# Half of the reciprocals in the preparation of the S4D modes become an exponential and a Newton step, and three scalings move from VectorE to ScalarE

## The chip, the cores and the metric

One core of one Trainium2 chip runs the whole kernel. Its engines are TensorE (PE, with its weight loads listed as PEld), VectorE (DVE), ScalarE (ACT), GpSimd (POOL) and SyncE (SP, which here only issues DMA transfers); each runs its own instructions in a fixed order and waits for the others through semaphores. The metric is the device time of one execution in microseconds (us), compared by the median of several runs.

## The reference, cut to what matters

The output is the sum of three terms over a layer-normalised input of 2048 tokens by 448 channels: the input itself, a diagonal state-space convolution (S4D), and a gated linear unit (GLU) with 1792 hidden columns.

```python
def _A_ref(u, log_A_real, A_imag, C_real, C_imag, log_dt, D_skip):
    dt = jnp.exp(log_dt)
    A = -jnp.exp(log_A_real) + 1j * A_imag
    C = (C_real + 1j * C_imag) * dt[:, None]
    P = jnp.exp((A * dt[:, None])[:, :, None] * pos[None, None, :])
    K = 2.0 * jnp.einsum("dn,dnl->dl", C, P).real
    ...                                   # y = causal convolution of u with K, by FFT
    return y + u * D_skip[None, None, :]

def _B_ref(x, w_gate, w_up, w_down):
    g = jnp.einsum("bsd,df->bsf", x, w_gate)
    u = jnp.einsum("bsd,df->bsf", x, w_up)
    return jnp.einsum("bsf,fd->bsd", _sigmoid(g) * u, w_down)

x = A_u
xn = _layernorm(x, axis=-1)
return x + _A_ref(xn, ...) + _B_ref(xn, ...)
```

There are 448 channels with 256 complex modes each. Of every mode the kernel needs a decay, exp(-x) with x = dt·exp(log_A_real), a phase per step, A_imag·dt/2π, and the magnitude and angle of C.

## The kernel before

Two streams of work are interleaved on one TensorE. `glu()` runs the GLU in groups of three (last: two) blocks of 128 hidden columns. For each block and each half `t` of the 1024 tokens in work it makes two accumulations of 12 matmuls (`gate`, line 698, tiles `gu`): three products of high and low parts, because 32-bit values are split in two. The tanh of the first (`th`, line 706, ACT), the product with the second (`hf`, line 709, DVE), its high part (`hh`, line 714, ACT) and low part (`hl`, line 716, DVE) follow. After a group come its down projections (`po`, line 811): eight accumulations, each drained by DVE into `acc` (line 816). `gu` and `po` share four PSUM banks, so the first four `gu` accumulations after a group of `po` each wait until DVE has drained one of the last four `po`. The weights of a block are loaded by SP (`wraw`), cast on ACT (`wh`, line 748) and their low part made on DVE (`wl`, line 752); there is one `wraw` buffer.

`conv()` first normalises the input, then prepares the modes (`prep`, two generators, h = 0 and 1, each with 224 channels as 112 partitions by 2·256 values, taken in turns), then generates the kernel K (`kgen`), and last works in the frequency domain (`spectra`). In `prep`, `exp` is an exponential of 514 columns on DVE, written as a polynomial (lines 311 to 318), whose last two columns are `dt`; `pieces` is a reciprocal on DVE in four pieces of 128 columns (line 322). It is called twice per half: on `m3`, for the angle of C, and on `pl` = 1 + tanh(x/2), from which line 373 makes exp(-x) - 1 = -2·tanh/(1 + tanh). `turn` transposes this on PE (line 431) and ACT copies it into `W` (line 433); the magnitudes of C go the same way into `GG`. The phases `U`, `V`, `T` are stored to DRAM as high (ACT, line 393) and low parts (POOL, line 398) by SP, and `phase_load` (line 481) brings them back for the first product of `kgen` (line 531, tile `tr`); `powers` (lines 443 to 448) starts `kgen`'s other input from `W`.

The order of instructions on each engine is not written by hand. A scheduler sets it when the program is built, from the order of emission, priorities (`hp`) and ties (`issue_after`, which puts an instruction behind another one); on the chip each engine then keeps that order, and an instruction that waits holds all behind it on its engine. ACT holds its functions in tables; the program loads one at its start, one for Arctan (line 363) and one at line 365, whose only purpose is to load the table for the rest of the run ahead of the sines.

## Time and profile before

| what | value |
|---|---|
| three timed runs | 732.49, 735.47, 735.87 us (median 735.47) |
| profiled execution, its own time | 737.56 us |
| its span in the trace | 735.7 us |
| mean granted TensorE clock | 0.974 of full speed |
| busy, share of the span | PE 92%, PEld 73%, DVE 76%, ACT 57%, POOL 49% |
| instructions | 19244 |

The span runs from the first to the last instruction; the execution's own time is 1.86 us longer. In a row of the timeline stand the start, the length, engine, line, operation, output<-inputs, the number of instructions merged, and in brackets how long the engine had been idle and what released it. Because consecutive instructions of one engine overlap a little, the time that one costs in a row of them is the distance of starts and not its length. In the table of stages each engine has its busy time and, in brackets, its instructions; behind them stand the granted TensorE clock, the busy share of the DMA engines and their GB/s.

### The profile page before, as it was taken

The page shows a single profiled execution, that of the slowest core. Times are in us where ns is not written, and L with a number is a line of the kernel's source. Part 1 is how long each engine was busy: PE and PEld are TensorE (multiplying, and loading weights), DVE is VectorE, ACT ScalarE, POOL GpSimd, SP SyncE. Part 2 cuts the span into 40 slices and gives each one's busy share as a digit, 9 for nine tenths or more (in the row PEclk, how much of TensorE's full clock was granted, in tenths as well). Part 3 has the DMA queues.
Part 4 walks back from the last instruction along what each step waited for, and adds up shares of the span by engine and source line. Part 5 has one row for each costly group of instructions (what it writes and reads, how often), then busy time and mean ns, then how long its engine had stood idle before and what let it go on. Part 6 is the DMA issues. An engine that isn't in the chain of part 4 may idle for free.

```text
span 735.7 us, 19244 instructions
## 1 busy us (share of the span) xinstructions
PE 680.4 (92%) x7780; PEld 535.5 (73%) x7780; DVE 560.1 (76%) x776; ACT 421.1 (57%) x654; POOL 360.6 (49%) x423
## 2 busy tenths in 40 slices
PE   2898699999999898899999999999999999989995
PEld 2676588878877787556778878877877777767783
DVE  5899995779889899778488988977955555555543
ACT  3656275479777778796686787677553322312320
POOL 2101076846987975776365697575943002530001
PEclk9998899999999999899999999999999999989998
DMA  9957155454334445456942332233259999997745
GB/s 205 230 147 205 29 165 158 162 172 151 84 111 153 144 118 163 133 151 190 261 141 83 103 109 89 82 112 98 63 162 302 252 243 255 249 263 161 194 120 157
DMA packets 102984, 117.24 MB, mean 159 GB/s; under 512 B 13232, under 2 KB 90864, under 8 KB 102896
## 3 DMA queue, kind: packets, MB, share of 16 engines
q1 hardware_dynamic: 78736, 91.87, 45.2%
q10 hardware_dynamic: 21584, 18.24, 9.3%
q0 software_dynamic: 2576, 5.90, 3.1%
q8 instruction: 61, 1.00, 0.6%
q14 instruction: 27, 0.22, 0.1%
HBM read 72.13 MB, written 43.84 MB: 158 GB/s over the span
## 4 chain that ended last, share of the span: by engine, by line
PE 63%; DVE 13%; DMA 7%; ACT 7%; issue 4%; SPq 3%; POOL 1%; ACTq 1%; POOLq 0%; DVEq 0%
PE gu L698 29%; PE po L811 11%; PE sp L893 7%; PE ko L605 5%; PE pv L920 4%; PE tr L531 3%; DVE Et L591 2%; DVE Ft L593 2%; DVE Et L592 2%; SPq L633 1%; ACT S L540 1%; ACT S L538 1%; DVE acc L816 1%; SPq L481 1%; DMA t<-in_c_t_dram 1%
## 5 line engine op out<-in xcount | busy, mean ns | idle before, releaser
L509 POOL TENSOR_TENSOR me<-me,pm 128x32 f32<-128x32 f32 (+1 forms) x168 | 140.3, 835 | 107.4 <-DVE Et L592 96.3
L509 POOL TENSOR_TENSOR mf<-mf,pm 128x64 f32<-128x64 f32 (+1 forms) x112 | 118.2, 1056 | 4.7
L698 PE MATMUL gu<-xh,wh 128*128 128x512 f32 x336 | 102.3, 412 | 7.0 <-DVE acc L816 6.1
L698 PE MATMUL gu<-xh,wl 128*128 128x512 f32 x336 | 98.9, 402 | 0.0
L698 PE MATMUL gu<-xl,wh 128*128 128x512 f32 x336 | 97.5, 396 | 0.0
L591 DVE TENSOR_TENSOR Et<-me,S 128x1024 f32<-128x1024 f32 x56 | 82.8, 1479 | 12.5 <-ACT S L540 10.8
L592 DVE TENSOR_TENSOR Et<-me,S 128x1024 f32<-128x1024 f32 x56 | 79.4, 1417 | 12.3 <-ACT me L522 9.6
L811 PE MATMUL po<-dh,hh 128*128 128x448 f32 x224 | 85.0, 380 | 3.9 <-DVE hf L709 3.1
L698 PEld LDWEIGHTS gu<-xh,wh 128*128 128x128 f32 x336 | 63.2, 195 | 28.9 <-DVE acc L816 6.5
L811 PE MATMUL po<-dl,hh 128*128 128x448 f32 x224 | 83.0, 371 | 0.0
L811 PE MATMUL po<-dh,hl 128*128 128x448 f32 x224 | 82.0, 369 | 0.0
L537 ACT ACTIVATE S<-tr 128x1024 f32<-128x1024 f32 x56 | 57.8, 1032 | 41.8 <-PE tr L531 41.2
L593 DVE TENSOR_TENSOR Ft<-mf,S 128x1024 f32<-128x1024 f32 x56 | 76.8, 1372 | 5.2 <-ACT S L540 2.7
L605 PEld LDWEIGHTS ko<-Et,Ft 128*32 128x32 f32 x3584 | 54.1, 110 | 32.8 <-issue 13.2
L605 PE MATMUL ko<-Et,Ft 128*32 128x64 f32 x3584 | 65.0, 221 | 12.3 <-DVE Ft L593 11.4
L698 PEld LDWEIGHTS gu<-xh,wl 128*128 128x128 f32 x336 | 65.1, 194 | 15.2 <-DVE pl L316 0.7
L698 PEld LDWEIGHTS gu<-xl,wh 128*128 128x128 f32 x336 | 64.5, 192 | 14.0
L714 ACT CAST hh<-hf 128x512 fp32r<-128x512 f32 x56 | 34.9, 623 | 64.5 <-DVE hf L709 58.6
L709 DVE SCALAR_TENSOR_TENSOR hf<-th,gu 128x512 f32<-128x512 f32 x56 | 38.1, 681 | 43.6 <-PE gu L698 39.5
L706 ACT ACTIVATE th<-gu 128x512 f32<-128x512 f32 x56 | 33.7, 602 | 64.4 <-PE gu L698 52.0
L540 ACT ACTIVATE S<-S,hpi 128x1024 f32<-128x1024 f32 x56 | 65.6, 1171 | 0.5 <-issue 0.3
L816 DVE SCALAR_TENSOR_TENSOR acc<-po,acc 128x448 f32<-128x448 f32 x80 | 48.0, 614 | 21.7 <-PE po L811 21.7
(206 smaller groups left out, 1295.6 us busy)
## 6 DMA issues: line engine op xcount, KB each, us to landing
sk_d<-sk ACTq DMA_DIRECT2D x14, 512.0 KB
sx<-x_d SPq DMA_DIRECT2D x32, 224.0 KB
skl<-sk_d SPq DMA_DIRECT2D x16, 448.0 KB
vp<-v_d SPq DMA_DIRECT2D x16, 448.0 KB
v_d<-vt SPq DMA_DIRECT2D x62, 112.0 KB
ph<-ph_d SPq DMA_DIRECT2D x224, 24.0 KB
wt_d<-wh SPq DMA_DIRECT2D x9, 512.0 KB
wt_d<-wl SPq DMA_DIRECT2D x9, 512.0 KB
```

Source lines behind the costliest of these rows:

```text
L509: ins = nc.gpsimd.tensor_tensor(m[:, :, w + a : 2 * w : n], m[:, :, a:w:n], par(base + i).unsqueeze(2).to_broadcast([128, 4 * DC, w // n]) ...
L537: nc.scalar.activation(rows(cs), pv, AF.Abs)
L540: sins[:] = [nc.scalar.activation(cs, cs, AF.Sin, scale=-TWO_PI, bias=hpi)]
L591: v.tensor_tensor(Et[:, :, :, 32:64], two(me[:, :, 32:64]), S[:, 1::-1], ALU.mult)
L592: v.tensor_tensor(Et[:, :, :, 0:32], two(me[:, :, 0:32]), S[:, 1:3, :, ::-1], ALU.mult)
L593: fts[:] = [v.tensor_tensor(Ft, two(mf), S[:, 3:5], ALU.mult)]
L605: mm = nc.tensor.matmul(ko[32 * j : 32 * j + 32, sl], Ft[:, cc, DC * h + 4 * q + j], Et[:, cc, DC * h + 4 * q + j], start=(k == 0), stop=( ...
L698: glu_mm[:] = [nc.tensor.matmul(ps, a_, b_, start=(n == 0), stop=(n == len(mm) - 1))]
L709: marks[1] = v.scalar_tensor_tensor(hf, th, 1.0, pgu[1], ALU.add, ALU.mult)
L811: glu_mm[:] = [nc.tensor.matmul(po, a_[:, bs], w_, start=(n == 0), stop=(n == 3 * fc - 1))]
L816: v.scalar_tensor_tensor(acc[:, b], po, 0.5, acc[:, b], ALU.mult, ALU.add)
L893: mm = nc.tensor.matmul(to, tb[:kk, t, 64 * c : 64 * c + 64], rhs, start=True, stop=True, skip_group_check=True,)
```

## The change

In both halves of `prep`:

- The reciprocal of 1 + tanh(x/2) goes. With t = tanh(x/2), 2/(1 + t) equals 1 + exp(-x), so ACT computes exp(-x) with `AF.Exp` and adds 1 (`rc`, in the buffer of `ki`), and DVE improves it by one Newton step (two instructions) before the last product.
- `dt` is scaled on ACT by four constants (`hdt`, now four pairs of columns), and ACT uses these as scales: for the tanh, the exponential, the phases (`aim`, was line 386) and the magnitudes (`a3`, was line 419).
- The first product of the polynomial (line 314) becomes an ACT instruction.
- Tanh and Exp are emitted earlier, in the section of `exp`, and Arctan is tied behind the last of them.

```diff
@@ exp
-        v.tensor_scalar(pl, fr, cs[7], None, ALU.mult)
+        nc.scalar.activation(pl, fr, AF.Identity, scale=cs[7])
@@ prep
-        hdt = pool.tile([CP, 2], F32, name="hdt", bufs=2)
+        hdt = pool.tile([CP, 4, 2], F32, name="hdt", bufs=2)
         part = lambda t, i: t[:, N * i : N * i + N]
-        dt = lambda i: ex[:, 2 * N + i : 2 * N + i + 1]
...
         yield from exp(ex, ki, fr, pl)
-        v.tensor_scalar(hdt, ex[:, 2 * N :], 0.5, None, ALU.mult)
+        for i, c in enumerate((0.5, -1.0, 1.0 / TWO_PI, 2.0)):
+            nc.scalar.activation(hdt[:, i], ex[:, 2 * N :], AF.Identity, scale=c)
+        fr, pl, ki = fr[:, : 2 * N], pl[:, : 2 * N], ki[:, : 2 * N]
+        rc = ki.bitcast(F32)
+
+        def scaled(to, src, c, func=AF.Identity):
+            for i in range(2):
+                nc.scalar.activation(part(to, i), part(src, i), func, scale=hdt[:, c, i : i + 1])
+
+        scaled(fr, ex, 0, AF.Tanh)
+        scaled(rc, ex, 1, AF.Exp)
+        nc.scalar.activation(pl, fr, AF.Identity, bias=one[:CP])
+        exps[:] = [nc.scalar.activation(rc, rc, AF.Identity, bias=one[:CP])]
         yield
...
-        nc.scalar.activation(w3, w3, AF.Arctan)
+        with tc.issue_after(exps[0].ins):
+            nc.scalar.activation(w3, w3, AF.Arctan)
...
-        fr, pl, ki = fr[:, : 2 * N], pl[:, : 2 * N], ki[:, : 2 * N]
-        for i in range(2):
-            nc.scalar.activation(part(fr, i), part(ex, i), AF.Tanh, scale=hdt[:, i : i + 1])
-        nc.scalar.activation(pl, fr, AF.Identity, bias=one[:CP])
-        pieces(pl)
-        v.scalar_tensor_tensor(pl, fr, -2.0, pl, ALU.mult, ALU.mult)
+        v.scalar_tensor_tensor(pl, pl, -0.5, rc, ALU.mult, ALU.mult)
+        v.scalar_tensor_tensor(rc, pl, 2.0, rc, ALU.add, ALU.mult)
+        v.scalar_tensor_tensor(pl, fr, -1.0, rc, ALU.mult, ALU.mult)
         yield
         turn(pl, W1s[0], h)
...
-        for i in range(2):
-            v.tensor_scalar(part(fr, i), part(aim, i), 1.0 / TWO_PI, dt(i), ALU.mult, ALU.mult)
+        scaled(fr, aim, 2)
         nc.scalar.copy(ki, fr)
...
-        for i in range(2):
-            v.tensor_scalar(part(a3, i), part(a3, i), 2.0, dt(i), ALU.mult, ALU.mult)
+        scaled(a3, a3, 3)
```

The scheduler's order moves with it. Line numbers of the changed kernel are 7 higher from `kgen` on, and differ in `prep`.

On DVE, around the last four drains of the first group of `po`, before (tiles ending in 377 and 389 are `a3` of h = 0 and 1):

```order
L417 TENSOR_TENSOR a_377<-a_377,b_378 112x512
L322 RECIPROCAL pl<-pl 112x128 x8
L816 SCALAR_TENSOR_TENSOR acc<-po,acc 128x448 x2
L417 TENSOR_TENSOR a_389<-a_389,b_390 112x512
L260 SCALAR_TENSOR_TENSOR z<-z,ve 128x8
L816 SCALAR_TENSOR_TENSOR acc<-po,acc 128x448 x2
```

and in the changed kernel, from the Newton step of h = 0 on (tiles ending in 380 and 392 are the angles `w3` of h = 0 and 1):

```order
L380 SCALAR_TENSOR_TENSOR pl<-pl,ki 112x512
L261 SCALAR_TENSOR_TENSOR ys<-z,ys 128x8
L381 SCALAR_TENSOR_TENSOR ki<-pl,ki 112x512
L263 SCALAR_TENSOR_TENSOR zs<-mv,ys 128x8
L382 SCALAR_TENSOR_TENSOR pl<-fr,ki 112x512
L380 SCALAR_TENSOR_TENSOR pl<-pl,ki 112x512
L385 SCALAR_TENSOR_TENSOR w_380<-w_380,s_381 112x512
L381 SCALAR_TENSOR_TENSOR ki<-pl,ki 112x512
L823 SCALAR_TENSOR_TENSOR acc<-po,acc 128x448 x3
L385 SCALAR_TENSOR_TENSOR w_392<-w_392,s_393 112x512
L382 SCALAR_TENSOR_TENSOR pl<-fr,ki 112x512
```

Before, the fifth to eighth drains stand behind eight reciprocals; now the fifth to seventh stand behind both halves' Newton steps and behind line 385, which needs the Arctan of h = 0 from ACT.

On ACT, the stretch with the two later table loads, before:

```order
L363 ACT_TABLE_LOAD
L363 ACTIVATE w_380<-w_380 112x512
L363 ACTIVATE w_392<-w_392 112x512
L296 COPY x1ab<-ko 128x448
L300 DMA x_d<-x1ab 64x2x448
L748 CAST wh<-wraw 128x1024
L296 COPY x1ab<-kp 128x448
L300 DMA x_d<-x1ab 64x2x448
L365 ACT_TABLE_LOAD
```

and now, from the scalings of `dt` of h = 1 on:

```order
L354 ACTIVATE hdt<-ex 112x2 x4
L300 DMA x_d<-x1ab 64x2x448
L364 ACTIVATE pl<-fr,one 112x512
L365 ACTIVATE ki<-ki,one 112x512
L360 ACTIVATE fr<-ex,hdt 112x256 x2
L360 ACTIVATE ki<-ex,hdt 112x256 x2
L364 ACTIVATE pl<-fr,one 112x512
L365 ACTIVATE ki<-ki,one 112x512
L375 ACT_TABLE_LOAD
L375 ACTIVATE w_380<-w_380 112x512
L375 ACTIVATE w_392<-w_392 112x512
L360 ACTIVATE fr<-aim,hdt 112x256 x2
```

The Arctans, ahead of the cast of a weight block before, now stand behind it and behind all scalings, tanhs and exponentials of both halves. There are three table loads in each program.

On SP, the end of the stores of phases (`w_380` and `w_392` are the low parts of the last phase of h = 0 and 1, which POOL makes one after the other) and the first loads of them, before:

```order
L399 DMA ph_d<-w_380 112x2x256
L394 DMA ph_d<-P_115 112x2x256
L633 DMA wraw<-in_B_w_gate_dram 64x128
L631 DMA wraw<-in_B_w_up_dram 128x3x128
L399 DMA ph_d<-w_392 112x2x256
L633 DMA wraw<-in_B_w_up_dram 64x128 x2
L639 DMA rd<-in_B_w_down_dram 128x448
L755 DMA wt_d<-wh 128x1024
L755 DMA wt_d<-wl 128x1024
L481 DMA ph_1103<-ph_d 12x2x256 x8
L481 DMA ph_1104<-ph_d 12x2x256 x8
```

and now:

```order
L407 DMA ph_d<-w_380 112x2x256
L640 DMA wraw<-in_B_w_up_dram 64x128 x2
L407 DMA ph_d<-w_392 112x2x256
L646 DMA rd<-in_B_w_down_dram 128x448
L762 DMA wt_d<-wh 128x1024
L488 DMA ph_1111<-ph_d 12x2x256 x8
L488 DMA ph_1112<-ph_d 12x2x256 x8
L762 DMA wt_d<-wl 128x1024
```

The last loads of the weight block `wraw` now stand ahead of the store of `w_392`, and the loads of phases ahead of the store of `wl`; both programs have the phase loads behind the store of `wh`.

More of the change, by code (lines that the diff above doesn't have):

```diff
@@ L1103, in s4d_glu_kernel @@
     xq, psc, raws, acl, marks, slots, pqs = list(x_first), [], [], [], [None, None], {}, []
-    W1s, GGs, act = [], [], []
+    W1s, GGs, act, exps = [], [], [], []
     gens = [conv(), glu()]
```

## The prediction

> **What bounds the kernel now.** I read the table of waits for TensorE first (the releaser, total us, times, longest), up to 120 us, because `prep` runs there.
>
> ```profile
> PE gu L698 <- DVE acc L816: 6.1, 1, 6.1
> PE po L811 <- DVE acc L816: 0.8, 1, 0.8
> ```
>
> TensorE waits twice for VectorE's drains of `po`, together 6.9 us. The table of stages tells whose fault that is:
>
> ```profile
> core 0: us, PE busy (x) PEld busy (x) DVE busy (x) ACT busy (x) POOL busy (x), PEclk, DMA share, GB/s
> 60.00:80.00 20.00, 16.11 (x78) 13.60 (x62) 19.73 (x39) 14.77 (x24) 0.20 (x1) 0.83 0.59 161
> 80.00:100.00 20.00, 13.92 (x52) 11.05 (x51) 19.57 (x37) 6.66 (x14) 2.62 (x2) 0.83 0.18 58
> 100.00:120.00 20.00, 20.00 (x97) 16.56 (x96) 14.31 (x15) 10.48 (x22) 15.44 (x14) 1.00 0.67 205
> 120.00:140.00 20.00, 20.00 (x112) 17.73 (x111) 15.98 (x25) 12.25 (x16) 17.26 (x21) 1.00 0.37 119
> ```
>
> From 60 to 100 us VectorE is full (39.3 of 40 us) and TensorE is not; ScalarE has 13 us free between 80 and 100. Behind 100 us TensorE is full. So 60 to 100 us is bound by VectorE, and what follows by TensorE. The timeline of VectorE, then of TensorE, shows the place:
>
> ```profile
> 73.14 0.61 DVE L816 SCALAR_TENSOR_TENSOR acc<-po,acc 128x448 f32<-128x448 f32 x1
> 76.69 0.61 DVE L816 SCALAR_TENSOR_TENSOR acc<-po,acc 128x448 f32<-128x448 f32 x1
> 80.30 6.62 DVE L322 RECIPROCAL pl<-pl 112x128 f32<-112x128 f32 x8
> 86.85 1.09 DVE L816 SCALAR_TENSOR_TENSOR acc<-po,acc 128x448 f32<-128x448 f32 x2
> ```
>
> ```profile
> 81.01 0.37 PE L811 MATMUL po<-dh,hl 128*128 128x448 f32 x1
> 87.46 1.65 PE L698 MATMUL gu<-xh,wh 128*128 128x512 f32 x3 [6.08 <-DVE acc L816]
> 93.51 0.39 PE L698 MATMUL gu<-xr,wh 128*128 128x512 f32 x1
> 95.36 0.84 PE L698 MATMUL gu<-xh,wh 128*128 128x512 f32 x3
> 96.03 0.39 PE L698 MATMUL gu<-xr,wh 128*128 128x512 f32 x1
> ```
>
> The fifth drain stands behind all eight reciprocals; the first `gu` needs its bank and starts 0.61 us after the drain begins. The wait costs more than 6.08 us: the 14 matmuls from 87.46 to 93.51 (rows between left out) take 6.05 us, while 3 take 0.67 us from 95.36 to 96.03, so 14 would take 3.1. Restarting slowly costs 2.9 us. (The waits of 0.8 us leave no such mark.)
>
> The Trainium skill, "TensorE: Matmul & The Clock Gate", Part 1, has the array at half clock until about 3.4 us of sustained work have passed; by it the slow start would cost 1.7 us and not 2.9. The stretch here is longer, and I keep the trace's 2.9.
>
> **VectorE, removed and added.** The costs of one in a run are distances of starts.
>
> ```profile
> L314 DVE TENSOR_SCALAR pl<-fr 112x514 f32<-112x514 f32 x2 | 0.8, 418 | 0.0
> L419 DVE TENSOR_SCALAR a<-a,ex 112x256 f32<-112x256 f32 x4 | 1.2, 341 | 0.0
> 90.72 1.28 DVE L373 SCALAR_TENSOR_TENSOR pl<-fr,pl 112x512 f32<-112x512 f32 x2
> 92.53 1.13 DVE L386 TENSOR_SCALAR fr<-aim,ex 112x256 f32<-112x256 f32 x4
> ```
>
> Gone: eight reciprocals 6.55 (80.30 to 86.85), two of line 314 0.7 (0.8 less overlap), four of line 386 1.05, four of line 419 1.15, together 9.45 us. New: four Newton instructions of the form of line 373, 1.21 a pair (90.72 to 91.93): 2.4 us. Net 7.0 us less on the engine that is full. Line 373 itself stays.
>
> **ScalarE, added, and now waited for.** What moves is long on ScalarE, and the new order puts the fifth to seventh drains behind line 385, which needs the first Arctan.
>
> ```profile
> 66.06 1.28 ACT L363 ACT_TABLE_LOAD   x1
> 67.36 0.63 ACT L363 ACTIVATE w<-w 112x512 f32<-112x512 f32 x1
> 71.62 0.20 ACT L365 ACTIVATE junk<-w 112x1 f32<-112x1 f32 x1
> 71.73 0.71 ACT L377 ACTIVATE m<-w,qpi 112x512 f32<-112x512 f32 x1
> 74.70 0.89 ACT L370 ACTIVATE fr<-ex,hdt 112x256 f32<-112x256 f32 x2
> 75.50 0.71 ACT L380 ACTIVATE w<-w,hpi 112x512 f32<-112x512 f32 x1
> 72.96 0.60 ACT L714 CAST hh<-hf 128x512 fp32r<-128x512 f32 x1
> 76.91 1.33 ACT L371 ACTIVATE pl<-fr,one 112x512 f32<-112x512 f32 x2
> ```
>
> ```profile
> 66.51 0.68 DVE L716 TENSOR_TENSOR hl<-hf,hh 128x512 fp32r<-128x512 f32 x1
> 68.63 0.69 DVE L318 SCALAR_TENSOR_TENSOR ex<-pl,ki 112x514 f32<-112x514 f32 x1
> ```
>
> The end of `exp` (line 318, twice 0.6 us) now follows directly on the `hl` of 66.51, so it ends at about 68.3; one polynomial instruction more ahead of that place pays for the two of line 314 gone. From there ScalarE has, until the first Arctan is done: eight scalings of `dt` at 0.11 (71.62 to 71.73; at most its length, 0.20): 0.9. Two pairs of Tanh at 0.80 (74.70 to 75.50), 1.6. Two pairs of Exp: no row shows an Exp; bounds are a pair of Tanh of the same shape, 0.80, and two 512-column instructions, 1.33; the first is the nearer, 1.6. Four additions of 1 at 0.62: 2.5. One `hh` cast: 0.6. Table load: 1.3 (66.06 to 67.36). Arctan: 0.6. Sum 9.1, so 77.4 us; eight of these read what ScalarE has just written, which I bound by 0 and 0.3 each and take at 0.1: 78.2 (77.4 to 80). Then VectorE does line 385 and one Newton instruction, 1.2, and the fifth drain begins at 79.4. TensorE may start `gu` 0.6 later, at 80.0 (to 82).
>
> TensorE itself comes there at 81.2 (81.01 plus one 0.2 step) less the 0.8 wait, since the first drains no longer stand behind lines 376, 416 and 379: 80.4. Four small transposes now come first, about 0.4, which it did later before. So the wait of 6.08 and that of 0.8 vanish, or leave up to 1.2 us, too short to be slow after. Gain on TensorE: 6.08 + 0.8 + 2.9 = 9.8, with an allowance of 0.5 for a rest: 9.3 us.
>
> On the other side, the Trainium skill, "ScalarE: Activation LUTs", What ACT_TABLE_LOAD costs, has 1.28 us for a load and 1.38 of draining besides. The rows show 1.30 from the start of the load to the next instruction. By the page the first Arctan would come 1.4 us later, the fifth drain at 80.8, and TensorE would wait some 0.5 us: the gain would be 8.8 for 9.3.
>
> The hidden parts: the four scalings of phases and magnitudes, 0.8 a pair on ScalarE, 3.2 in all, fall into the 13 us that it has free between 80 and 100; without that cover they would delay the phases by as much. The cast of the next block's weights needs the buffer of the block that starts here, four accumulations of 12 steps of 0.227 us or 11 us after the start, and is no earlier wanted.
>
> **What is late next.** `kgen`'s start must come forward as well, or TensorE meets its first product (`tr`) too early.
>
> ```profile
> 94.16 1.83 DVE L401 TENSOR_TENSOR aim<-fr,ki 112x512 f32<-112x512 f32 x2 [0.43 <-ACT ki L387]
> 98.54 3.92 POOL L398 TENSOR_TENSOR aim<-aim,p 112x512 fp32r<-112x512 f32 x2 [3.70 <-DVE fr L405]
> 109.26 1.15 POOL L775 TENSOR_TENSOR dl<-rd,dh 128x448 fp32r<-128x448 f32 x1
> 110.37 1.74 POOL L398 TENSOR_TENSOR w<-w,P 112x512 fp32r<-112x512 f32 x1
> 112.49 1.11 SPq L633 DMA_DIRECT2D wraw<-in_B_w_up_dram  x2
> 115.37 1.05 ACT L748 CAST wh<-wraw 128x1024 fp32r<-128x1024 f32 x1 [4.75 <-DMA wraw<-in_B_w_up_dram]
> 118.12 7.82 SPq L481 DMA_DIRECT2D ph<-ph_d  x16
> ```
>
> POOL makes the low phases without a break from 98.54 to 112.1. On SP the last weights wait for its last but one and last result, the cast at 115.37 for them, the store of `wh` for the cast, and the phase loads for that store. VectorE is 7.0 us less busy but now waits about 2 us for ScalarE around the Arctan, and each later hand-over costs up to 0.43 (94.16); I take 5.5 us earlier for POOL (0 to 7). In the new order the weights stand ahead of the last store, so they wait for one POOL instruction less and for the `dl` ahead of it (109.26 to 112.1): 2.9 us more. So phases come 8.4 us earlier (3 to 10), about what TensorE gains. If the change stopped there, the lesser, 8.4, is what reaches 140 us.
>
> **What reaches the end.** The rest of every engine's order stays almost the same, so later stages shift as a whole, where nothing else bounds them.
>
> ```profile
> PE ko L605 <- DVE Ft L593: 11.1, 10, 2.2
> ```
>
> ```profile
> 220.00:260.00 40.00, 35.98 (x507) 29.14 (x506) 37.59 (x40) 31.12 (x47) 33.49 (x33) 0.96 0.49 155
> ```
>
> From 100 to 520 us TensorE waits 11.1 us for VectorE's `Ft`; these waits depend on how the streams meet and may take some of the gain. I leave 0.9 us for that: 7.5 us. In the profiled execution's terms 735.7 goes to 728.2 (its own time 737.56 to 730.1). The profiled run lies 2.1 us above the median of the timed ones, so I subtract from the median: 735.47 - 7.5 = 728.0.
>
> **Rivals.**
> - ScalarE takes VectorE's place. If the self-waits cost 0.3 and more and the scalings of `dt` 0.2, the Arctan ends near 82, `gu` starts near 84, TensorE waits over 3 us and starts slowly again (2.9). Left: 87.5 - 84 + 0.8 = 4.3, or 731.2. For it: the chain is serial and one instruction late holds three drains. Against: every duration in it stands in a row.
> - The gain is real but taken back by `kgen`, whose VectorE is near full at 220 to 260 us (37.6 of 40), POOL at 33.5: if the 11.1 us of `Ft` waits grow by half, 5.5, then 2 us remain: 733.5. Against: those streams start earlier too.
> - Slower: the hand-overs between ScalarE and VectorE in the phases' chain. VectorE's order from line 385 to line 416 and ScalarE's from the second table load on wait for each other some 25 times where both were loosely coupled. At 0.43 apiece that is 10.8 us against the 7.0 saved; TensorE then stands at `tr` until the phases come, some 4 us later than before, slow start (2.9) included 6: 741.5. It decides from 0.3 us each, if nothing overlaps. Against: most of them have other work in between.
> - That the change does not do what it says: an Exp outside Tanh's table would add loads. Both programs have three. No chance of its own.
>
> **Chances and range.** Forecast 0.65, with its own range 725.5 to 731; ScalarE's chain 0.16; taken back 0.12; slower 0.07. A measurement of this kernel tells 0.5%, or 3.7 us, from no change, so 731.8 and 739.1 are the bounds. Faster: nearly all of the forecast and about two thirds of the next, 0.75. Slower: 0.06. The same: 0.19. The range goes from 725.0, where TensorE's 9.8 us arrive whole, to 733.5 and leaves out about 0.15.
>
> **What would show it.** Right: no wait of `gu` for `acc` over 1 us near 81 us; first `gu` at 80.4 to 82; TensorE at full clock from 80 to 100; the first Arctan done near 78; `ph` loads near 110; three table loads; every later stage some 8 us earlier. Wrong: VectorE idle before line 385 until 81 or later with TensorE waiting on `acc`; `tr` waiting for `ph`; or a stage behind 140 us that takes longer than before.

## The result, and the profile after

| what | before | after |
|---|---|---|
| timed runs, median (range) | 733.98 us (731.60 to 737.25, 6 runs) | 723.93 us (722.09 to 728.76, 6 runs) |
| ratio, with its 95% interval | | 0.9857 (0.9824 to 0.9889) |
| profiled execution, its own time (span) | 737.56 us (735.7) | 724.73 us (722.9) |
| busy DVE, ACT, PE | 560.1, 421.1, 680.4 us | 553.6, 428.6, 676.9 us |
| mean granted TensorE clock | 0.974 | 0.980 |

The change makes the kernel 10 us faster. Medians here and below leave out three executions that took 950 us and more (two of e13, one of the kernel before). The forecast was 728.0 us, 7.5 us less, in a range that began at 725.0: the direction was right and the gain too small.

The table of TensorE's waits up to 120 us, after (releaser, total us, times, longest), no longer has `acc` in it:

```profile
PE po L818 <- DVE hf L716: 2.9, 1, 2.9
PE po L818 <- ACT hh L721: 1.4, 1, 1.4
```

The table of stages, after:

```profile
60.00:80.00 20.00, 17.09 (x77) 15.23 (x72) 17.45 (x36) 14.79 (x33) 0.20 (x1) 0.83 0.57 153
80.00:100.00 20.00, 20.00 (x96) 16.57 (x96) 20.00 (x28) 17.93 (x38) 10.11 (x5) 1.00 0.38 115
100.00:120.00 20.00, 18.28 (x81) 14.56 (x80) 14.38 (x24) 11.40 (x21) 13.62 (x19) 1.00 0.54 162
```

Between 80 and 100 us TensorE was busy for 13.92 us at a clock of 0.83; now it is busy for all 20.00 at full clock. VectorE stays full there, but with other work. The timelines of ScalarE, VectorE and TensorE, after, at the place of the old wait:

```profile
73.91 0.90 ACT L360 ACTIVATE ki<-ex,hdt 112x256 f32<-112x256 f32 x2
...
76.06 1.28 ACT L375 ACT_TABLE_LOAD   x1
77.35 1.15 ACT L375 ACTIVATE w<-w 112x512 f32<-112x512 f32 x2
```

```profile
78.01 0.69 DVE L385 SCALAR_TENSOR_TENSOR w<-w,s 112x512 f32<-112x512 f32 x1 [1.25 <-ACT w L375]
78.62 0.69 DVE L381 SCALAR_TENSOR_TENSOR ki<-pl,ki 112x512 f32<-112x512 f32 x1
79.22 1.68 DVE L823 SCALAR_TENSOR_TENSOR acc<-po,acc 128x448 f32<-128x448 f32 x3
```

```profile
79.90 0.96 PE L705 MATMUL gu<-xh,wh 128*128 128x512 f32 x3
...
83.20 0.39 PE L705 MATMUL gu<-xr,wh 128*128 128x512 f32 x1
```

The first Arctan is done at 78.0, line 385 and one Newton instruction follow, the fifth drain starts at 79.22, and TensorE starts `gu` 0.68 us after it without a gap, 7.56 us earlier than before (87.46) and at full pace. On SP's queue the loads of the phases, after, start 7.8 us earlier than before (118.12):

```profile
110.30 7.77 SPq L488 DMA_DIRECT2D ph<-ph_d  x16
```

So the two times that the forecast is added up from came out nearly to the microsecond. What it missed lies elsewhere. This table follows three landmarks (starts of instructions of VectorE, from the traces; `Ft` is line 593 before, `yy` line 904) through two profiles of each kernel, the second ones from the runs e8 and e7:

| us | first `Ft` | 21st `yy` | last `yy` | from 21st to last `yy` | span |
|---|---|---|---|---|---|
| before, first | 132.8 | 640.1 | 706.4 | 66.4 | 735.7 |
| before, second | 134.0 | 640.6 | 706.8 | 66.2 | 735.9 |
| after, first | 124.5 | 632.6 | 694.0 | 61.4 | 722.9 |
| after, second | 124.3 | 631.0 | 693.8 | 62.7 | 722.6 |

Up to 640 us the change gains 8.5 us (means of the two); from there to the last `yy` another 4.2, in a stage of `spectra` that the diff does not touch: from the 21st `yy` on every engine has the same instructions in the same order in both traces. The first profile of before shows what happens in it, on VectorE, on GpSimd, and on TensorE:

```profile
641.54 0.39 DVE L907 TENSOR_TENSOR yy<-pd 128x224 f32<-128x224 f32 x1
...
648.73 0.98 DVE L906 TENSOR_TENSOR yy<-yy 128x224 f32<-128x224 f32 x1
649.74 2.43 DVE L907 TENSOR_TENSOR yy<-pd 128x224 f32<-128x224 f32 x1
...
652.63 0.61 DVE L905 TENSOR_TENSOR pd<-kc,sp 128x448 f32<-128x448 f32 x1
```

```profile
648.43 1.04 POOL L758 CAST wh<-wraw 128x1024 fp32r<-128x1024 f32 x1 [6.20 <-PE sp L893]
649.55 2.37 POOL L759 TENSOR_TENSOR wl<-wraw,wh 128x1024 fp32r<-128x1024 f32 x1
```

```profile
653.38 1.72 PE L955 MATMUL pv<-vp,wf 64*32 64x224 f32 x16 [2.67 <-DVE pd L905]
655.03 1.65 PE L698 MATMUL gu<-xh,wh 128*128 128x512 f32 x3
...
659.89 0.92 PE L698 MATMUL gu<-xh,wh 128*128 128x512 f32 x3
```

Line 907 takes 0.39 us by itself. Where POOL subtracts at the same time it takes 2.43 and ends 0.25 us after POOL does (652.17 and 651.92). `pd` stands behind it, TensorE waits 2.67 us for `pd` and then works slowly until about 660. In the first profile after, POOL meets the same products:

```profile
642.57 0.61 DVE L912 TENSOR_TENSOR pd<-kc,sp 128x448 f32<-128x448 f32 x1
643.11 1.21 DVE L913 TENSOR_TENSOR yy<-yy 128x224 f32<-128x224 f32 x1
...
644.77 2.05 DVE L914 TENSOR_TENSOR yy<-pd 128x224 f32<-128x224 f32 x1
```

```profile
643.03 1.04 POOL L765 CAST wh<-wraw 128x1024 fp32r<-128x1024 f32 x1 [7.03 <-DMA wraw<-in_B_w_up_dram]
644.16 2.42 POOL L766 TENSOR_TENSOR wl<-wraw,wh 128x1024 fp32r<-128x1024 f32 x1
```

But here the last `pd` has started before POOL does, and TensorE does not wait. In this profile GpSimd's cast waits for its weights to land (the releaser in brackets; in the first profile of before its wait ended with TensorE's `sp`), while TensorE comes when its own stream gets there; the two meet or miss each other.

### The profile page after: what moved, and what is told of

Read it like the earlier page. It is cut to its first block, busy times and chain, and to the rows that moved or that the text cites. A ratio compares the mean times of both kernels' runs of the same rounds, so it can differ in the third digit from the quotient of the medians.

```text
span 722.9 us, 19254 instructions
## 1 busy us (share of the span) xinstructions
PE 676.9 (94%) x7780; PEld 532.5 (74%) x7780; DVE 553.6 (77%) x760; ACT 428.6 (59%) x678; POOL 361.9 (50%) x423
## 4 chain that ended last, share of the span: by engine, by line
PE 63%; DVE 11%; ACT 9%; DMA 6%; issue 4%; SPq 2%; POOL 2%; ACTq 1%; POOLq 0%; DVEq 0%
PE gu L705 27%; PE po L818 14%; PE sp L900 7%; PE ko L612 5%; PE pv L927 4%; PE tr L538 3%; DVE Ft L600 2%; DVE Et L599 2%; DVE Et L598 2%; ACT S L547 1%; ACT S L545 1%; ACT S L544 1%; SPq L640 1%; DVE pm L452 1%; DMA ph<-ph_d 1%
## 5 line engine op out<-in xcount | busy, mean ns | idle before, releaser
L516 POOL TENSOR_TENSOR me<-me,pm 128x32 f32<-128x32 f32 (+1 forms) x168 | 138.2, 823 | 104.4 <-DVE Et L599 87.9
L516 POOL TENSOR_TENSOR mf<-mf,pm 128x64 f32<-128x64 f32 (+1 forms) x112 | 121.1, 1081 | 4.7
L705 PE MATMUL gu<-xh,wh 128*128 128x512 f32 x336 | 100.8, 407 | 0.9 <-ACT xh L221 0.7
L705 PE MATMUL gu<-xh,wl 128*128 128x512 f32 x336 | 97.3, 397 | 0.0
L600 DVE TENSOR_TENSOR Ft<-mf,S 128x1024 f32<-128x1024 f32 x56 | 78.7, 1405 | 5.6 <-ACT S L547 2.7
L723 DVE TENSOR_TENSOR hl<-hf,hh 128x512 fp32r<-128x512 f32 x56 | 47.7, 851 | 18.2 <-ACT hh L721 18.2
```

Source lines behind the costliest of these rows:

```text
L516: ins = nc.gpsimd.tensor_tensor(m[:, :, w + a : 2 * w : n], m[:, :, a:w:n], par(base + i).unsqueeze(2).to_broadcast([128, 4 * DC, w // n]) ...
L600: fts[:] = [v.tensor_tensor(Ft, two(mf), S[:, 3:5], ALU.mult)]
L705: glu_mm[:] = [nc.tensor.matmul(ps, a_, b_, start=(n == 0), stop=(n == len(mm) - 1))]
L723: v.tensor_tensor(hl, hf, hh, ALU.subtract)
```

## The experiments

All times are medians of the timed runs; each batch had its own runs of the kernel before on the same chip.

| run | what | us | before | ratio (95%) |
|---|---|---|---|---|
| e1 | Newton alone | 732.16 | 733.41 | 0.9973 (0.9947 to 0.9999) |
| e2 | eight reciprocals left out | 727.79 | 733.41 | 0.9912 (0.9883 to 0.9941) |
| e3 | before, late `wl` on VectorE | 737.68 | 733.41 | 1.005 (1.0027 to 1.0074) |
| e4 | after, the same | 729.17 | 733.41 | 0.9937 (0.9905 to 0.997) |
| e5 | scalings alone | 733.29 | 734.89 | 0.9975 (0.9951 to 1.0) |
| e6 | after, reciprocals tied | 723.89 | 734.89 | 0.9857 (0.9826 to 0.9888) |
| e7 | after, again | 724.11 | 734.89 | 0.9864 (0.9824 to 0.9903) |
| e8 | before, again | 733.45 | 734.89 | 0.9996 (0.9972 to 1.0019) |
| e9 | before, late `wl` in four | 735.11 | 734.53 | 0.9993 (0.9963 to 1.0023) |
| e10 | after, the same | 726.26 | 734.53 | 0.9874 (0.9836 to 0.9911) |
| e11 | after, Arctan later | 725.22 | 734.53 | 0.9873 (0.9833 to 0.9913) |
| e12 | e6 and e10 together | 725.19 | 734.53 | 0.986 (0.9815 to 0.9904) |
| e13 | e9, stores off ScalarE | 732.53 | 734.75 | 0.9987 (0.9955 to 1.0019) |
| e14 | e10, stores off ScalarE | 723.45 | 734.75 | 0.9846 (0.9805 to 0.9887) |
| e15 | e12, stores off ScalarE | 724.32 | 734.75 | 0.9844 (0.9801 to 0.9887) |

### e1, e2, e5: the parts of the change, one at a time

e1 has the exponential and the Newton step, and with them the earlier Tanh and Exp and the tie of the Arctan; line 314 and the scalings stay on VectorE. The core of it:

```diff
...
-        pieces(pl)
-        v.scalar_tensor_tensor(pl, fr, -2.0, pl, ALU.mult, ALU.mult)
+        v.scalar_tensor_tensor(pl, pl, -0.5, rc, ALU.mult, ALU.mult)
+        v.scalar_tensor_tensor(rc, pl, 2.0, rc, ALU.add, ALU.mult)
+        v.scalar_tensor_tensor(pl, fr, -1.0, rc, ALU.mult, ALU.mult)
```

> Only the reciprocal is replaced (Exp on ScalarE, one Newton step); line 314 and all scalings stay on VectorE. VectorE loses 6.55 - 2.4 = 4.2 us of work instead of 7.0. Theory A (the place: what is gained is TensorE's wait for the drains behind the reciprocals, 6.9 us, and its slow restart, 2.9): the wait of gu for acc near 81 us is gone and the gain is that of the whole change, 8 to 11 us against before. Theory B (the amount of work on the full engine): 4.2/7.0 of the gain, about 6 us.

e2 is the kernel before without the reciprocals of `pl` (the decay is then not divided by 1 + t).

```diff
-        pieces(pl)
```

> The kernel before with the eight reciprocals of 1 + tanh left out (the modes' decay is then wrong), everything else left; ScalarE gets no new work and no drain stands behind the Arctan. Theory A: no wait of gu for acc near 81 us, a gain of 8 to 11 us as in the change, so the longer chain on ScalarE costs nothing. Theory B: 6.6 us. If ScalarE's chain cost the change something, this kernel would be faster than the change by 1 us or more.

e5 moves only line 314 and the scalings to ScalarE; the reciprocals stay.

```diff
-        v.tensor_scalar(pl, fr, cs[7], None, ALU.mult)
+        nc.scalar.activation(pl, fr, AF.Identity, scale=cs[7])
...
-            v.tensor_scalar(part(fr, i), part(aim, i), 1.0 / TWO_PI, dt(i), ALU.mult, ALU.mult)
+        scaled(fr, aim, 2)
...
-            v.tensor_scalar(part(a3, i), part(a3, i), 2.0, dt(i), ALU.mult, ALU.mult)
+        scaled(a3, a3, 3)
...
```

> Only the scalings by dt (and line 314) go to ScalarE; all sixteen reciprocals stay on VectorE. Theory A (what reaches the later stages is the lesser of two advances, that of the first gate products after the drains and that of the phases' last stores; both follow VectorE's work ahead of them): VectorE has 0.7 + 1.05 + 1.15 = 2.9 us less, of which the 0.7 and the first scaling stand ahead of the fifth drain, so TensorE still waits at least 4.5 us for it near 81 us, starts slowly again, and the time falls by 1 to 3 us, ratio 0.996 to 0.999. Theory B (the 4 us that the whole change gains beyond leaving the eight reciprocals out come from the scalings alone): the time falls by 4 us or more, ratio 0.9945 or less. Theory C (ScalarE's longer chain costs what VectorE saves): ratio 1.000 or above.

Measured: 1.3, 5.6 and 1.6 us off the medians, where the whole change takes off 10. e1 gains far less than either sum for it; e2's 5.6 is nearer to its second sum, 6.6. The timelines of e1 on TensorE, on SP, on VectorE and on ScalarE, and its stage from 140 us on (compare the row of before behind it), tell why:

```profile
78.74 0.86 PE L708 MATMUL gu<-xh,wh 128*128 128x512 f32 x3
```

```profile
115.05 6.50 SPq L491 DMA_DIRECT2D ph<-ph_d  x16
```

```profile
118.46 1.23 DVE L762 TENSOR_TENSOR wl<-wraw,wh 128x1024 fp32r<-128x1024 f32 x1 [2.39 <-ACT wh L758]
```

```profile
123.19 0.83 ACT L458 ACTIVATE pm<-pm,one 128x640 f32<-128x640 f32 x1 [1.84 <-DVE pm L455]
...
125.01 0.99 ACT L547 ACTIVATE S<-tr 128x1024 f32<-128x1024 f32 x1
```

```profile
140.00:180.00 40.00, 36.83 (x498) 29.37 (x500) 38.53 (x42) 30.21 (x45) 29.49 (x30) 0.96 0.53 173
```

```profile
140.00:180.00 40.00, 39.85 (x454) 32.26 (x453) 32.68 (x37) 28.73 (x43) 20.25 (x25) 1.00 0.49 156
```

TensorE starts `gu` at 78.74, even earlier than in the whole change, but the phases come only 3.1 us earlier (115.05 for 118.12), and a third input of `kgen`, the powers (tile `pm`), not at all. On VectorE half of them stand behind `wl`, which waits 2.39 us for its cast; the first ten are done at 123.15, for 122.99 before. ScalarE waits for them and takes up what `tr` brings (`tr` starts at 121.72) only at 125.01. From 140 to 180 us TensorE then loses 3 us of work in waits, and the 21st `yy` is 1.3 us earlier than in the first profile of before (638.7 for 640.1). e2 leaves another one behind, on SP and on TensorE:

```profile
107.91 6.43 SPq L480 DMA_DIRECT2D ph<-ph_d  x16
```

```profile
74.06 0.47 PE L810 MATMUL po<-dh,hh 128*128 128x448 f32 x1 [1.75 <-DVE acc L815]
...
82.69 0.94 PE L697 MATMUL gu<-xh,wh 128*128 128x512 f32 x3
```

The phases come 10.2 us earlier, but `gu` only 4.8, since without the new order of VectorE the drains still stand behind other work of the preparation (1.75 us wait, `gu` at 82.69); the 21st `yy` is 5.4 us earlier than there (634.6). In e5 the drains stand behind both sets of reciprocals, `gu` starts later than before, at 88.39, and the 21st `yy` is 0.5 us earlier; the median lies within what the first theory expected. Side by side, with e11 from below (us earlier than in the first profile of before; the powers by the end of their first ten instructions on VectorE):

| run | first `gu` | phase loads | powers | 21st `yy` |
|---|---|---|---|---|
| e1 | 8.7 | 3.1 | -0.2 | 1.3 |
| e2 | 4.8 | 10.2 | 8.2 | 5.4 |
| e5 | -0.9 | 2.7 | 1.8 | 0.5 |
| e11 | 8.9 | 3.7 | 5.8 | 5.6 |
| the change | 7.6 | 7.8 | 7.2 | 7.4 |

What arrives is close to the least of the three advances; in e11 it is 1.9 us more. The prediction had counted the first two alone, and these do not tell e1 from e11: `gu` and phases agree within 0.6 us, the powers are 6.0 apart and the 21st `yy` 4.3. The parts together are worth more (10) than one by one (1.3 and 1.6), because each alone leaves at least one of the three behind.

### e3, e4: the late subtraction moved to VectorE

```diff
-                            nc.gpsimd.tensor_tensor(wl, raw, wh, ALU.subtract)
+                            v.tensor_tensor(wl, raw, wh, ALU.subtract)
```

> The kernel before, with the low parts of the reloaded weights of the second half (line 759, five instructions) made on VectorE instead of POOL, so that no POOL instruction of 2.4 us can slow VectorE's products at 650 us. Theory A says that 5.0 of the 12.8 us between the two profiled executions come from there and not from the preparation: no wait of pv there over 1 us, 731 to 733 us, that is 0 to 4 us below the runs of before of the same chip, and less spread. Rival: the 5 us are not a matter of chance but come with the earlier preparation; then this kernel stays at before's time.

> The changed kernel with the same edit of line 759. Theory A: 721 to 724 us, 8 to 10 us below the kernel before with this edit (e3_late_before), which is what the preparation alone is worth: 9.8 us on TensorE less what later waits take. Rival (the late 5 us belong to the change): 12 us or more below it.

Measured: 4.3 us more than before, and 5.2 more than the change; both times are above what was expected, and the two kernels are 8.5 us apart, as the first theory had it. The edit does not take the collision away but puts a wait in its place; VectorE and TensorE of e3:

```profile
653.67 1.23 DVE L759 TENSOR_TENSOR wl<-wraw,wh 128x1024 fp32r<-128x1024 f32 x1 [7.55 <-POOL wh L758]
```

```profile
656.11 3.51 PE L955 MATMUL pv<-vp,wf 64*32 64x224 f32 x48 [5.87 <-DVE pd L905]
```

VectorE now stands 7.55 us for POOL's cast, which waits for the weights, and TensorE 5.87 us for what is queued behind. The trial says nothing about the collision itself, only that this stage charges what VectorE loses there.

### e7, e8: both kernels once more

No edit; a second profile and more times of each.

> The changed kernel unaltered, once more, for a second profile and more times. Theory A (the stage near 650 us loses about 4.5 us in those executions in which POOL's subtraction for the low weights of the second half falls on VectorE's products for pv, by chance of the transfers): times in two groups some 4 us apart as the kernel before has them; the landmarks of this profile agree with those of the first within 1 us up to 640 us, whichever group it is in; a TensorE wait over 1.5 us near 645 to 650 us stands in the profile only if it is in the upper group. Mean ratio 0.986 to 0.990. Theory B (the change moves the two apart for good): one group of times, ratio 0.984 to 0.986.

> The kernel before unaltered, for a second profile. Ratio 1.000 within 0.003. Theory A (the stage near 650 us differs by execution): if this profile's time lies near 732, TensorE has no wait over 1 us for pv near 653 us and the last 80 us are some 4 us shorter than in the first profile; if it lies near 737 the wait of 2.67 us is there again. Theory B (the wait is a fixed part of the kernel before, and the two groups of times come from elsewhere): the wait is there at either time.

The landmarks stand in the table above: up to 640 us the two profiles of a kernel agree within 1.2 us (before) and 1.6 us (after). e8's profile, at 737.82, has the wait again, TensorE:

```profile
654.24 1.72 PE L955 MATMUL pv<-vp,wf 64*32 64x224 f32 x16 [2.94 <-DVE pd L905]
```

Over all batches there are 109 runs of the kernel before, 729.8 to 740.1 us, with a median of 734.28, and 12 of the changed kernel, 721.47 to 730.65, with a median of 724.11. Their spreads are alike, the difference of medians is 10.2 us. The rival's one narrow group of times for the changed kernel is not there. Both profiles of before (737.56, 737.82) lie in the slower quarter of its runs, both of the change (724.73, 724.40) near its median; so some 3 of the 13 us between the spans are how the executions fell.

### e9, e10: the late subtraction in four pieces

```diff
-                            nc.gpsimd.tensor_tensor(wl, raw, wh, ALU.subtract)
+                            for i in range(4):
+                                nc.gpsimd.tensor_tensor(wl[:, :, i], raw[:, :, i], wh[:, :, i], ALU.subtract)
```

> The kernel before, with POOL's subtraction for the low weights of the second half (one instruction of 2.37 us) in four of a quarter of the size; TensorE's, VectorE's and ScalarE's order stays the same. Theory A (in the slower executions near 650 us VectorE's products for pv stand still for as long as one instruction of POOL on the same memory lasts): line 907 takes at most 0.39 + 0.7 us there for 2.43, TensorE's wait for pv falls under 1.5 us, the upper group of times (736 and more) thins out or goes, median 731.5 to 732.5, ratio 0.995 to 0.998. Theory B (VectorE stands still until POOL is done with all four): nothing changes, ratio 0.999 to 1.002. Theory C (it was the transfers, not POOL): as B, but line 907 keeps its 2.4 us even where no POOL instruction runs.

> The changed kernel with the same split. If theory A of the split holds: one group of times near 723 (the three in twelve of 726 and more go), ratio to the kernel before 0.984 to 0.986, and against the split kernel before 9 us less, which is then what the change is worth where neither collides (7.5 was forecast). If the change owes over 3 us of its gain to rarer collisions: only 6 to 7 us less than the split kernel before. If the split does nothing: 724 with the two groups as before.

Measured: no gain in either kernel. In neither profile do the pieces meet the products, so what they cost there isn't shown; but e9 is slow in its profile all the same (738.27 us, 66.5 us from the 21st to the last `yy`), from another wait. ScalarE and TensorE of e9:

```profile
658.46 4.26 ACTq L240 DMA_DIRECT2D out_dram<-ac  x3
662.76 0.60 ACT L706 ACTIVATE th<-gu 128x512 f32<-128x512 f32 x1 [12.93 <-DMA out_dram<-ac]
...
664.64 0.96 ACT L927 COPY vt<-pv 128x448 f32<-128x448 f32 x2
```

```profile
665.22 1.76 PE L894 MATMUL sp<-skl,tb 128*64 128x224 f32 x8 [3.75 <-ACT vt L927]
```

Three output stores are issued on ScalarE's queue and take 4.26 us; `th` and the copy `vt` stand behind them, and TensorE waits 3.75 us for the bank that `vt` frees. The same wait stands in e12 (3.29 us), in e2 (2.98), and in the second profile after (1.68). A theory of one collision near 650 us falls: there are at least two waits, and an execution meets the one, the other or (e10, with 1.5 and 1.4 us) both.

### e13, e14, e15: both late waits taken away

To the four pieces comes that SyncE and GpSimd alone issue the first output stores (`out` takes the engines as its last argument):

```diff
...
-                    out(ac[:, 4 * q : 4 * q + 4], 4 * q, h)
+                    out(ac[:, 4 * q : 4 * q + 4], 4 * q, h, (nc.sync, nc.gpsimd))
```

> The kernel before with both late waits taken away that the profiles show between 640 and 665 us: POOL's subtraction in four pieces, and the first output stores issued by SyncE and GpSimd alone, so that ScalarE's th and vt no longer stand behind three of them (1.7 to 4.3 us of issue). Theory A (the last stage is the same work in both kernels and differs only by these two waits): from the 21st yy to the last one 60.5 to 62 us for 66.4, and one narrower group of times, median 729.5 to 731.5, ratio 0.993 to 0.997. Theory B (the stores or the pieces only move the wait to SP or POOL): 63 us and more in that stage, ratio 0.998 to 1.003.

> The changed kernel with the same two edits. Theory A (the change is worth what is gained before 640 us, 8.4 us in the mean of the profiles, and what the timed runs show beyond that is how the last stage falls): the last stage as long as in the freed kernel before within 1 us, the time 8 to 9 us under that of the freed kernel before. Theory B (the last stage profits from the change by itself, since all of TensorE's work comes earlier against POOL's weight loads): the last stage 1.5 us and more shorter than in the freed kernel before, the time 10 us or more under it. Against the kernel before: ratio 0.981 to 0.984 under A, if the edits free the stage.

> The same two edits with the tie of the second half's reciprocals behind the last hf. The tie gave 1.7 us more up to the first Ft and gave it back by the twentieth (-8.4 against -8.4 of the change at 265 us). If it is worth nothing: the time of the freed changed kernel within 1.5 us. If it is worth its 1.0 to 1.7 us: under it by as much, ratio 0.979 to 0.982.

From the 21st to the last `yy` e13 takes 61.9 us and e14 60.6 (66.4 and 61.4 in the first profiles). The waits of `sp` are gone; e13 has in TensorE's timeline a third one instead, 1.93 us at 651.85 for a transfer (`vp<-v_d`).

The medians are 732.53 and 723.45, 9.1 us apart; with the pieces alone (e9, e10) they are 8.9 apart, as they stand 10.2. That is nearer to the first theory, 8 to 9 us before 640 us and the rest by chance, than to the second, but the intervals of the ratios (some 0.4% to either side, 3 us) leave 1 us undecided. Neither free kernel is measurably faster than its own kernel without the edits.

### e6, e12: an attempt to gain more

The changed kernel still waits 2.9 us for `hf` near 63 us, which stands behind the second half's reciprocals. A tie holds them back:

```diff
-        pieces(m3)
+        with tc.issue_after(hfs[-1].ins) if h == 1 else nullcontext():
+            pieces(m3)
```

> The changed kernel, with the second half's reciprocals of line 391 held back until the last hf of the first rows is made (one tie, nothing else written differently). In the changed kernel TensorE waits 2.9 us near 63 us for that hf and then works slowly for some us. Theory A (this stage is bound by VectorE's order, and TensorE's wait there is worth its length and the slow start): the wait falls under 1 us; if the modes' chain is not later by it, time 719 to 722, ratio 0.979 to 0.984. Theory B (the drains and phases that follow wait for the reciprocals, so the time is only moved): TensorE waits for the fifth drain near 80 us by as much, up to 3 us, and the time is that of the changed kernel within 1.5 us, ratio 0.984 to 0.988. Theory C: phases later by over 3 us, so that the time is above the changed kernel's, ratio 0.990 or more.

> The changed kernel with the tie of the second half's reciprocals behind the last hf and with the split together, as the candidate for the fastest. If the tie's gain up to the first Ft (1.7 us more than the change) reaches the end and the split removes the collisions: 721 to 722.5, ratio 0.982 to 0.984. If the tie only moves time (the first trial had the same median as the change) but the split works: 723, ratio 0.985. If neither: 724, ratio 0.986 to 0.987.

The tie takes one microsecond off that wait (1.90 us in e6, at 61.42, for 2.91). The first `Ft` comes at 122.7 for 124.4, but the 21st `yy` at 632.2, inside the 631.0 to 632.6 of the change: given back on the way. e6's profile (728.85 us) has the collision too, in a kernel with the change in it: TensorE waits 2.41 us for `pd` and the last stage takes 65.8 us. 723.89, 725.19 and 724.32 us (e6, e12, e15) are the time of the change: the second theory's number, though the time is lost between the first and the nineteenth `Ft` and not at the fifth drain.

### e11: the chain on ScalarE made longer

```diff
+        for _ in range(4 if h == 1 else 0):
+            exps[:] = [nc.scalar.copy(rc, rc)]
```

> The changed kernel with four copies of the second half's Exp result onto itself (0.6 us each, 2.4 to 2.8 us) ahead of the Arctan; VectorE's order then has the fifth to seventh drains ahead of what needs the Arctan. Theory A (the phases have no slack: what the later stages gain is the lesser of the drains' and the phases' advance): TensorE does not wait for the drains near 80 us, the phases' loads start 2.5 to 5 us later than 110.3, and the landmarks behind 150 us are 3 to 6 us ahead of the kernel before for 8, ratio 0.989 to 0.994. Theory B (the phases have some us to spare, the drains alone set the gain): ratio as the changed kernel's, 0.985 to 0.987. Theory C (TensorE waits for the drains after all and restarts slowly): ratio 0.992 to 0.997 with a wait on acc over 2 us.

VectorE's order has the drains ahead of the Arctan here, and TensorE starts `gu` at 78.53. Line 385 comes at 82.07 for 78.01, and SP and TensorE show what follows:

```profile
114.44 6.78 SPq L490 DMA_DIRECT2D ph<-ph_d  x16
```

```profile
105.26 0.98 PE L707 MATMUL gu<-xh,wh 128*128 128x512 f32 x3 [2.67 <-DVE hf L718]
...
120.23 0.71 PE L540 MATMUL tr<-sel,ph 128*128 128x512 f32 x2 [1.42 <-DMA ph<-ph_d]
```

The phases are 4.1 us later than in the change, and TensorE waits for them where it did not. The 21st `yy` comes at 634.4, 2.6 us behind the change, and the median is 725.22, 1.1 behind it. The landmarks fit the first theory (at its edge), the ratio lies between the two theories. So the phases' advance counts, but something like 1.5 us of it was to spare; how much of the 2.6 us the wait for `hf` (2.67 us) took, and how much the phases, is not separated.

## Why the direction was right and the size wrong

- **What bounds the kernel: right.** With VectorE relieved, TensorE runs through from 80 to 100 us at full clock; waits and slow restart are gone.
- **VectorE's 7.0 us: right.** Its busy time falls by 6.5 us (560.1 to 553.6). (By starts, 90.19 to 90.72 and 91.93 to 92.45, the four of line 419 cost 1.05 us and not 1.15.)
- **ScalarE's chain: right.** First Arctan done forecast for 78.2, found at 78.0; fifth drain 79.4 and 79.2; `gu` 80.4 and 79.9. VectorE waits for ScalarE 0.69 and 1.25 us there, for the 2 taken. In part errors cancel: the inputs came some 0.8 us earlier in this execution (the first wait of TensorE was 13.0 us before and 12.1 after), so that `exp` ended at 67.5 and not at 68.3, but ScalarE, busy with a cast of weights and a copy, began the scalings of `dt` only at 68.61. From there to 78.0 are 9.4 us, between the sum without self-waits, 9.1, and with them, 9.9. An Exp costs what a Tanh does: the pair of 73.91 takes 0.79 us to the next start, for the 0.80 taken. Three table loads, none added.
- **The slow restart: right.** The 14 matmuls from the first `gu` on take 3.30 us (79.90 to 83.20) where they took 6.05, and 3.32 for 6.03 in the second profiles: 2.7 us less, for the 2.9 taken from the row. The Trainium skill, "TensorE: Matmul & The Clock Gate", Part 1, has half clock until about 3.4 us of sustained work have passed; the 1.7 us estimated from that are further off. The Trainium skill, "ScalarE: Activation LUTs", What ACT_TABLE_LOAD costs, has 1.38 us of draining besides a load; the load of 76.06 is followed by the Arctan 1.29 us later, so the trace decides for the row there too.
- **Phases 8.4 us earlier: the sum right, its terms in part by luck.** The loads start 8.5 us earlier, in the mean of two profiles each (118.12 and 119.35 before, 110.30 and 110.11 after). These are SP's rows before, then SP's and POOL's after:

```profile
116.45 0.35 SPq L755 DMA_DIRECT2D wt_d<-wh  x1
117.71 0.32 SPq L755 DMA_DIRECT2D wt_d<-wl  x1
```

```profile
105.47 1.19 SPq L640 DMA_DIRECT2D wraw<-in_B_w_up_dram  x2
...
109.85 0.34 SPq L762 DMA_DIRECT2D wt_d<-wh  x1
```

```profile
102.82 2.98 POOL L406 TENSOR_TENSOR w<-w,P 112x512 fp32r<-112x512 f32 x2
```

  POOL is done with the low phases 6.6 us earlier, in the mean of two profiles each (at 112.11 and 105.80 in the first ones), where 5.5 were taken. The new place of the weights was taken at 2.9 us and gave 0.7: their last loads went out 0.4 us behind POOL's end and now go out 0.3 ahead of it, since `dl` no longer stands between POOL's last two results. The remaining 1.2 us were not in the sum: the phase loads no longer stand behind the store of `wl`, and follow that of `wh` by 0.45 us for 1.67. That 6.6 + 0.7 + 1.2 comes so near to 5.5 + 2.9 is luck.
- **The lesser of two advances counts: right here, but not the whole rule.** e2 and e5 show it within 1.5 us, e1 shows a third input that the sum had left out, and e11 that the rule is not sharp. In the change the powers came 7.9 us earlier as well (mean of two profiles each), which was not worked out beforehand.
- **"What reaches the end": here the prediction failed.** It took 0.9 us off for later waits on `Ft`, let every later stage shift as a whole, and so came to 7.5. Of the waits nothing was charged: 11.1 us before, and after, in the table of waits from 100 to 520 us:

```profile
PE ko L612 <- DVE Ft L600: 11.4, 10, 2.3
```

  At 640 us 8.5 us of gain are still there, 1.0 more than forecast (8.6 in the mean of five profiles of each kernel, with e3, e9, e13 and e4, e10, e14, whose edits act only from about 510 us on). Behind that the sum had no term at all. The last stage is no block that shifts as a whole: GpSimd waits for its weights, ScalarE for the issue of the output stores, TensorE follows its own stream, and where they meet costs up to 6 us (60.6 to 66.5 us in the profiles of this study, e3 left out). The difference of the medians, 10.2, less 8.5 leaves 1.7 us. That this stage differs so much between executions is shown; that the change gains anything there by itself is not. The interval of the ratio, 0.9824 to 0.9889, is a gain of 8.1 to 12.9 us and holds 8.5, and the kernels with the same edit in the late stage are 8.5 (e3, e4), 8.9 (e9, e10) and 9.1 us (e13, e14) apart.
- **The base.** The 7.5 us were taken from 735.47, the median of three runs; 109 runs have 734.28. That is 1.2 us of the miss. The sum: 1.2 for the base, 1.0 for the stages up to 640 us and 1.7 that stay open make 3.9, which is 728.0 less 724.1. So the mechanism held up to 640 us, and what was mis-sized is the base and this last step: 0.9 us charged that nothing took, and no term for a stage that varies by 6 us.
- **The rivals.** None came. ScalarE did not take VectorE's place (no wait for `acc`); the `Ft` waits did not grow beyond 0.3 us; the hand-overs did not make the phases later. (The slower rival's own sum is off: 4 and 2.9 us are 6.9 and not 6, so 742.4.)
- **The range** was to reach down to where TensorE's 9.8 us arrive whole; from its base that is 725.7, and 725.0 stands there. It took in the unknown costs of the edit, and not how much the kernel itself varies: 10 us between the fastest and the slowest of its runs.

## What to carry to other kernels

When a stage has several inputs, list them all, work out the advance of each and count the least; a part of an edit that leaves one of them behind looks worthless alone (1.3 and 1.6 us here) and may be worth much together with the other part. A late stage in which engines meet by the timing of transfers doesn't shift as a whole: compare two profiles of the same kernel before taking a difference there for the edit's. And take the base from as many runs as there are; where times spread by over 1%, the median of three and the one profiled execution can each be off by microseconds.

## What the hardware showed beyond that

- A VectorE instruction whose inputs both lie in SBUF stands still while GpSimd works on SBUF, and ends 0.24 to 0.25 us after GpSimd's does: 0.38 became 0.98 and 0.39 became 2.43 us (above). A product with an input in PSUM does not: in the first profile of before `pd`, which reads `sp` from PSUM, starts inside POOL's `wl` and keeps its 0.61 us, and the `yy` behind it, 0.38 us by itself, does not:

```profile
562.60 0.61 DVE L905 TENSOR_TENSOR pd<-kc,sp 64x448 f32<-64x448 f32 x1
563.13 1.32 DVE L906 TENSOR_TENSOR yy<-yy 64x224 f32<-64x224 f32 x1
```

```profile
561.85 2.36 POOL L759 TENSOR_TENSOR wl<-wraw,wh 128x1024 fp32r<-128x1024 f32 x1
```

  The Trainium skill, "SBUF — State Buffer", Who interferes with whom, has just this: GpSimd shares a pair of ports with VectorE, and whoever comes first keeps it for a whole instruction. The trace agrees.
- Issuing three output stores kept ScalarE's queue for 4.26 us in e9 (above) and for 1.71 in the first profile of before (at 655.46); what stands behind them waits as long.
- How a wait of TensorE is paid for afterwards is not set by its length alone. After 2.41 us (e6) three `gu` take 1.65 us, and full pace is back only at about 652; after 2.67 us in the first profile of before they take 1.65 as well (655.03, above), and after 2.67 us in e11 (above) 0.98, near full pace.

```profile
645.30 1.60 PE L963 MATMUL pv<-vp,wf 64*32 64x224 f32 x16 [2.41 <-DVE pd L913]
646.84 1.65 PE L706 MATMUL gu<-xh,wh 128*128 128x512 f32 x3
```
